# Two attention blocks on one core: wider exponentials, four-way PE tiles, exponentials by bit pattern, and orders written by a list scheduler

## The chip, the cores and the metric

The kernel runs on one core of one Trainium2 chip. The metric is the device time of one execution in microseconds (us), the median of the runs shown. The core has five engines with a queue each: PE (TensorE: matmuls, and the loading of weights, PEld), ACT (ScalarE), DVE (VectorE), POOL (GpSimd) and SP (SyncE, which here only issues DMAs). Matmuls write PSUM, which has eight banks of 512 float32 columns by 128 partitions.

## The reference, cut to what matters

Two independent attention blocks read 2048 tokens of width 448, with 16 heads of 28 columns, and their outputs are put side by side.

```python
# A: full attention, one key and one value head shared by all 16 query heads
q = (x @ wq).reshape(1, 2048, 16, 28).transpose(0, 2, 1, 3)
k, v = x @ wk, x @ wv
p = softmax(einsum("bhqd,bkd->bhqk", q, k) * 28 ** -0.5)
a = einsum("bhqk,bkd->bhqd", p, v) ... @ wo
# B: each token sees itself and 7 earlier tokens, two apart
idx = pos[:, None] - 2 * arange(8)[None, :]
logits = where(idx >= 0, q . k[idx] * 28 ** -0.5, -1e9)
b = (softmax(logits) . v[idx]) ... @ wo
out = concatenate([a, b], axis=-1)
```

A has 16 heads x 2048 queries x 2048 keys of scores. Laid out as keys on 128 partitions by 512 queries, one PSUM bank each, these are 1024 banks, and every one of their elements needs an exponential.

## The kernel before

The program is built by hand. A method adds items with a key (a period number and a rank), all items are sorted by key, and the sorted list gives each engine its order. Waits are written out item by item.

**A.** The loop has 512 periods p (`NPER`), one for each block of 128 keys (`tb`), pair of heads (`pair`) and chunk of 512 queries (`sc`). In a period PE makes the scores of two heads (`QK`, L693: two matmuls with 30 rows of the array each, at row positions 32 apart, into two banks). ACT takes the exponential of both banks in one instruction (`EXP`, L709, 128x1024) into one of three buffers `expT`. PE multiplies that by the values (`PV`, L730: two matmuls of 32 output rows at column positions 32 apart), which adds into one of two banks. The value tile has a column of ones, so row 28 collects the sum of the exponentials. Six of the eight banks belong to this loop: two slots of two banks for the scores, two for `PV`. Two rows beside the 28 of each head carry a bound on the score, taken from the squares of queries and keys, so that no exponential overflows.

The order on PE within a period is: wait for the last exponential (`FILLWAIT`), one step of other work or a filler, `PV(p-1)`, `QK(p+1)`. The other work (`_XTask`, `schedule_x`) has banks 6 and 7 and is placed by deadline: the query projections for the next chunk (L545), the projections of B (L621), the output projections (L853 for A, L1083 for B). Where nothing is due, `filler_item` (L1175) issues a matmul of the identity whose result nobody reads.

**B.** PE projects B's queries, keys and values (L621), DVE evicts them (L637), and the keys and values go to a scratch tensor in DRAM and come back eight times, shifted by two rows each (L911), so that all eight keys of a token lie on the token's own partition. Everything else is elementwise on DVE, in 16 blocks of 128 tokens: eight products (L930), four sums over the 28 columns (L940), maximum, subtraction, an exponential on ACT (L978), the weights, products with the values (L1004, L1012) and sums (L1031 to L1038). PE then transposes the result (L1056) and projects it.

**Start and end.** Before the loop, SP issues four transposing DMAs of A's input (L303) and, behind them on the same queue, the weights (L326 to L330). PE makes values, keys and the first queries, the bound is worked out, and the loop begins. After each chunk the sums go through small DMAs to 16 partitions (`den_sc`, L756), DVE takes the reciprocal (L769), PE spreads it (L811), DVE multiplies (L821), and the outputs are projected and stored.

Of the kernel before, what the change touches and what calls it, by code (L numbers as in the profile page):

```python
# [10 lines left out]
I32 = mybir.dt.int32  # L11

S = 2048
D = 448
H = 16
DH = 28
NSB = S // 128
SCALE = float(DH) ** -0.5
WIN = 8
NEG = -1.0e9  # L20

NSC = 4
NPAIR = 8
NTB = 16
NPER = NSC * NPAIR * NTB
NGRP = NSC * NPAIR

BANKW = 512
NWARM = 10
XGAP = 6  # L30


NKV = 2


def P1B(k):
    return 42 + 26 * k


class _Sem:  # L40
    def __init__(self, h, name):
        self.h = h
        self.name = name
        self.count = 0


class _Eng:

    def __init__(self, gen, name, engine):
        self.gen = gen  # L50
        self.name = name
        self.engine = engine
        self.thunks = []

    def w(self, sem, count):
        if count is None or count <= 0:
            return
        assert count <= sem.count, (
            f"{self.name}: wait on {sem.name}>={count} but only {sem.count} signalled so far (global order violation)"
        )  # L60
        eng = self.engine
        h = sem.h
        self.thunks.append(lambda: eng.wait_ge(h, count))

    def i(self, fn, sig=None, inc=1):
        eng = self.engine
        if sig is None:
            self.thunks.append(lambda: fn(eng))
            return None
        sig.count += inc  # L70
        h = sig.h
        self.thunks.append(lambda: fn(eng).then_inc(h, inc))
        return sig.count


class _XTask:
    def __init__(self, name, kinds, elig, deadline, slot_fn):
        self.name = name
        self.kinds = kinds
        self.nslots = len(kinds)  # L80
        self.elig = elig
        self.deadline = deadline
        self.slot_fn = slot_fn
        self.deps = []
        self.slots = []
        self.bank = None
        self.st = {}


class _Gen:  # L90
    def __init__(self, nc, A_x, A_wq, A_wk, A_wv, A_wo, B_x, B_wqkv, B_wo, out):
        self.nc = nc
        self.A_x, self.A_wq, self.A_wk, self.A_wv, self.A_wo = A_x, A_wq, A_wk, A_wv, A_wo
        self.B_x, self.B_wqkv, self.B_wo = B_x, B_wqkv, B_wo
        self.out = out
        self.items = []
        self._seq = 0

    def add(self, key, fn):
        self._seq += 1  # L100
        self.items.append((key, self._seq, fn))

    def sem(self, es, name):
        return _Sem(es.enter_context(self.nc.semaphore(name=name)), name)

    def bank(self, b, lo=0, n=BANKW):
        return self.ps[:, b * BANKW + lo: b * BANKW + lo + n]

    def bank_rows(self, b, r0, r1, lo=0, n=BANKW):
        return self.ps[r0:r1, b * BANKW + lo: b * BANKW + lo + n]  # L110

    def bank_bf(self, b, lo=0, n=2 * BANKW):
        return self.psb[:, b * 2 * BANKW + lo: b * 2 * BANKW + lo + n]

    def build(self):
        nc = self.nc
        with ExitStack() as es:
            self.alloc(es)
            self.plan()
            self.items.sort(key=lambda t: (t[0], t[1]))  # L120
            for key, seq, fn in self.items:
                fn()
            block = es.enter_context(nc.Block())
            E = self.E

            @block.gpsimd
            def _(eng):
                for t in E["gp"].thunks:
                    t()

            @block.sync
            def _(eng):
                for t in E["sp"].thunks:
                    t()

            @block.tensor
            def _(eng):
                for t in E["pe"].thunks:
                    t()

            @block.scalar
            def _(eng):
                for t in E["act"].thunks:
                    t()

            @block.vector
            def _(eng):
                for t in E["dve"].thunks:
                    t()

    def alloc(self, es):
# [5 lines left out]
        self.ps = es.enter_context(nc.psum_tensor("ps", [128, 8 * BANKW], FP32))  # L157
        self.psb = self.ps[:, :].bitcast(BF16)
        self.kv_dram = nc.dram_tensor("kv_scratch", (S, 2 * D), BF16)
# [3 lines left out]
        self.wqkv = sb([128, 4, 3 * D], BF16, "wqkv")  # L163
        self.qkv_q = sb([128, NSB, D], BF16, "qkv_q")
        self.kv_stage = sb([128, 2, 2 * D], BF16, "kv_stage")
        KS = WIN * 2 * D
        self.ARENA = NKV * KS + 2 * 8 * D + 6 * D
        self.arena = sb([128, self.ARENA], BF16, "arena")
        self.kT_rep = sb([128, S], BF16, "kT_rep")
        self.q_sq = sb([128, 4, 512], BF16, "q_sq")  # L170
        self.q_tmp = sb([128, 4, 512], BF16, "q_tmp")
        self.v_aug = sb([128, NTB, 32], BF16, "v_aug")
        self.qT = sb([128, 2, 4, 512], BF16, "qT")
        self.expT = sb([128, 3, 1024], BF16, "expT")
        self.PV_sb = sb([128, 2, 4, 512], FP32, "PV_sb")
        self.bsel4 = sb([16, 4, 128], BF16, "bsel4")
        self.oTn = sb([128, 2, 4, 512], BF16, "oTn")
        self.den_sc = sb([16, 2, 512], FP32, "den_sc")
        self.rden = sb([16, 512], FP32, "rden")
        self.rden_bf = sb([16, 512], BF16, "rden_bf")  # L180
        self.kmax = sb([128, 4], FP32, "kmax")
        self.cols = sb([128, 8], FP32, "cols")
        self.cols_i = sb([128, 1], I32, "cols_i")
        self.wq_pad = sb([128, 4, 512], BF16, "wq_pad")
        self.wq_raw = sb([128, 4, D], BF16, "wq_raw")
        self.wk4 = sb([128, 4, 128], BF16, "wk4")
        self.wv_pad = sb([128, 4, 32], BF16, "wv_pad")
        self.wo4 = sb([128, 4, D], BF16, "wo4")
        self.wo_B = sb([128, 4, D], BF16, "wo_B")
        self.ident = sb([128, 128], BF16, "ident")  # L190
        self.halfblk = sb([128, 128], BF16, "halfblk")
        self.ones8 = sb([128, 128], BF16, "ones8")
        self.mask_add = sb([128, H, WIN], FP32, "mask_add")
        self.lg = sb([128, H, WIN], FP32, "lg")
        self.lgm = sb([128, H, WIN], FP32, "lgm")
        self.lg2 = sb([128, 2, H, WIN], FP32, "lg2")
        self.mx = sb([128, H], FP32, "mx")
        self.e_t = sb([128, 2, H, WIN], FP32, "e_t")
        self.ssum = sb([128, H], FP32, "ssum")
        self.rs = sb([128, H], FP32, "rs")  # L200
        self.a_n = sb([128, H, WIN], BF16, "a_n")
        self.o_bf = sb([128, 8, D], BF16, "o_bf")
        self.oT_sb = sb([128, 3, 512], BF16, "oT_sb")
        self.outB = sb([128, 2, D], BF16, "outB")
        self.outA = sb([128, 2, D], BF16, "outA")

        ar = self.arena
        self.KV = [ar[:, r * KS:(r + 1) * KS].rearrange("p (w c) -> p w c", w=WIN) for r in range(NKV)]
        self.Ksh = [kv[:, :, 0:D] for kv in self.KV]
        self.Vsh = [kv[:, :, D:2 * D] for kv in self.KV]  # L210
        o = NKV * KS
        self.prod = ar[:, o:o + 8 * D].rearrange("p (w c) -> p w c", w=8)
        o += 8 * D
        self.prod2 = ar[:, o:o + 8 * D].rearrange("p (w c) -> p w c", w=8)
        o += 8 * D
        self.S4 = ar[:, o:o + 4 * D].rearrange("p (w c) -> p w c", w=4)
        self.S2 = ar[:, o + 4 * D:o + 6 * D].rearrange("p (w c) -> p w c", w=2)
        o += 6 * D
        assert o == self.ARENA, o
        self.kT_raw = ar[:, 1 * KS: 1 * KS + S]  # L220
        self.k_sq = ar[:, 1 * KS + S: 1 * KS + S + 4 * 512].rearrange("p (t c) -> p t c", t=4)
        assert 1 * KS + S + 4 * 512 <= 2 * KS

        self.sem_xa = self.sem(es, "in_xa")
        self.sem_xb = self.sem(es, "in_xb")
        self.sem_wa = self.sem(es, "in_wa")
        self.sem_wb = self.sem(es, "in_wb")
        self.sem_wo = self.sem(es, "in_wo")
        self.pe_qk = self.sem(es, "pe_qk")
        self.pe_pv = self.sem(es, "pe_pv")  # L230
        self.pe_x = self.sem(es, "pe_x")
        self.act_a = self.sem(es, "act_a")
        self.act_x = self.sem(es, "act_x")
        self.dve_a = self.sem(es, "dve_a")
        self.dve_b = self.sem(es, "dve_b")
        self.dve_x = self.sem(es, "dve_x")
        self.gp_s = self.sem(es, "gp_s")
        self.gp_b = self.sem(es, "gp_b")
# [1025 lines left out]
```

## Time and profile before

| | us |
|---|---|
| runs | 627.05, 628.19, 627.03; median 627.05 |
| span of the profiled execution | 627.4 (0.35 above the median) |
| first exponential of the loop starts | 59.3 |
| last wait for the sums before the final outputs (DMA `den_sc`) | 606.4 to 608.1 |
| PE busy / ACT busy / DVE busy / POOL busy | 549.7 / 507.3 / 360.3 / 22.3 |

One page of the profile shows one execution. "Busy" is the time covered by an engine's instructions; a matmul's end is modelled, so a PE that is busy all the time need not be at its best. A line of the groups gives the source line, the engine, what it writes and reads, its shape and count, then busy time and mean duration of one, then the idle time of the engine just before them and what ended it. The chain follows the work that ended last back to the start. The mean clock granted to PE was 0.986.

### The profile page before, as it was taken

To read this page: it belongs to the slowest core of one execution; us is meant where nothing else is said; L and a number is where in the kernel's file an instruction comes from. 1 tells how busy PE (TensorE), PEld (TensorE's weight loads), DVE (VectorE), ACT (ScalarE), POOL (GpSimd) and SP (SyncE) were. 2 spreads that over 40 slices of the span, in tenths; PEclk is the share of its full clock that TensorE was granted. 3 is DMA by queue.
4 is the path that set the end of the run, shared out by engine and by line. 5 is a ranking of instruction groups with operands and counts; after the bars stand their busy time and mean duration, and the time that the engine had idled before them with its cause. 6 is when DMAs were issued, how large, how long until landed. Compare 5 with 4: busy or idle time off the path is not lost.

```text
span 627.4 us, 7987 instructions
## 1 busy us (share of the span) xinstructions
PE 549.7 (88%) x2831; PEld 167.4 (27%) x2878; DVE 360.3 (57%) x600; ACT 507.3 (81%) x538; POOL 22.3 (4%) x42
## 2 busy tenths in 40 slices
PE   0295999999999998999999989999999999999956
PEld 0121222222222222222222222222222222222312
DVE  2114114687656767885766777777665977521135
ACT  0032888898888889998889999989989999999950
POOL 5006200000000000000000000000000000000000
PEclk9997999999999999999999999999999999999987
DMA  9920030430124043030223140303314030000001
GB/s 198 150 52 11 29 109 35 132 113 20 45 91 147 16 132 118 1 117 2 68 87 98 43 140 2 117 32 110 112 37 139 9 126 15 16 30 16 16 8 59
DMA packets 46461, 43.89 MB, mean 70 GB/s; under 512 B 22943, under 2 KB 46087, under 8 KB 46423
## 3 DMA queue, kind: packets, MB, share of 16 engines
q1 hardware_dynamic: 45447, 41.39, 22.7%
q0 software_dynamic: 976, 2.01, 1.3%
q8 instruction: 22, 0.36, 0.2%
q14 instruction: 16, 0.13, 0.1%
HBM read 31.72 MB, written 7.34 MB: 62 GB/s over the span
## 4 chain that ended last, share of the span: by engine, by line
PE 66%; ACT 21%; issue 4%; DVE 4%; SPq 3%; DMA 1%; ACTq 0%; DVEq 0%
ACT expT L709 21%; PE ps L730 20%; PE ps L693 19%; PE ps L621 8%; PE ps L1175 7%; PE ps L1083 3%; PE ps L853 2%; SPq L303 2%; PE ps L545 2%; PE ps L455 1%; PE ps L472 1%; PE ps L433 1%; PE ps L1056 1%; SPq L326 1%; DVE lg L940 1%
## 5 line engine op out<-in xcount | busy, mean ns | idle before, releaser
L709 ACT ACTIVATE expT<-ps 128x1024 bf16<-128x1024 f32 x512 | 498.7, 1022 | 56.0 <-PE ps L693 52.9
L730 PE MATMUL ps<-expT,v_aug 128*32 128x512 bf16 x1024 | 201.2, 389 | 23.0 <-ACT expT L709 13.3
L693 PE MATMUL ps<-qT,kT_rep 30*128 30x512 bf16 x1024 | 198.8, 385 | 0.0
L1175 PE MATMUL ps<-kT_rep,ident 128*128 128x512 bf16 x216 | 84.2, 390 | 9.9 <-ACT expT L709 8.8
L730 PEld LDWEIGHTS ps<-expT,v_aug 128*32 128x32 bf16 x1024 | 49.2, 92 | 136.6 <-ACT expT L709 70.2
L693 PEld LDWEIGHTS ps<-qT,kT_rep 30*128 30x128 bf16 x1024 | 48.3, 91 | 116.1 <-issue 116.1
L940 DVE TENSOR_REDUCE lg<-arena 128x32 f32<-128x896 bf16 x64 | 66.6, 1079 | 0.5
L621 PE MATMUL ps<-wqkv,xT_B 128*128 128x448 bf16 x192 | 58.0, 360 | 0.0
L1012 DVE TENSOR_TENSOR arena<-arena,a_n 128x1344 bf16<-128x1344 bf16 (+1 forms) x32 | 56.7, 1784 | 0.0
L637 DVE CAST kv_stage<-ps 128x448 bf16<-128x448 f32 x32 | 19.9, 622 | 45.5 <-PE ps L621 45.4
L1175 PEld LDWEIGHTS ps<-kT_rep,ident 128*128 128x128 bf16 x256 | 24.6, 96 | 69.2 <-ACT expT L709 53.3
L930 DVE TENSOR_TENSOR arena<-qkv_q,arena 128x448 bf16<-128x448 bf16 x128 | 40.8, 383 | 0.0
L749 DVE COPY PV_sb<-ps 64x512 f32<-64x512 f32 x32 | 21.8, 681 | 22.3 <-PE ps L730 21.6
L637 DVE CAST qkv_q<-ps 128x448 bf16<-128x448 f32 x16 | 10.0, 625 | 38.8 <-PE ps L621 38.8
L433 PE MATMUL ps<-wv_pad,xT_A 128*128 128x32 bf16 x64 | 5.4, 198 | 27.8 <-DVE cols L379 27.8
L438 ACT ACT_TABLE_LOAD x1 | 1.3, 1283 | 33.3 <-PE ps L433 33.3
L865 DVE CAST outA<-ps 128x448 bf16<-128x448 f32 x16 | 10.0, 623 | 29.9 <-PE ps L853 29.7
L1094 DVE CAST outB<-ps 128x448 bf16<-128x448 f32 x16 | 10.0, 622 | 29.7 <-PE ps L1083 29.6
L621 PEld LDWEIGHTS ps<-wqkv,xT_B 128*128 128x128 bf16 x192 | 14.5, 96 | 31.5 <-issue 30.8
L1083 PE MATMUL ps<-wo_B,oT_sb 128*128 128x448 bf16 x64 | 22.2, 374 | 0.3 <-DVE outA L865 0.3
L853 PE MATMUL ps<-wo,oTn 128*128 128x448 bf16 x64 | 21.3, 371 | 0.0
L769 DVE RECIPROCAL rden<-den_sc 16x512 f32<-16x512 f32 x4 | 13.4, 3338 | 9.9 <-DMA den_sc<-PV_sb 9.9
(86 smaller groups left out, 242.7 us busy)
## 6 DMA issues: line engine op xcount, KB each, us to landing
arena<-kv_scratch SPq DMA_DIRECT2D x121, 224.0 KB, 3.8
kv_scratch<-kv_stage SPq DMA_DIRECT2D x16, 224.0 KB, 1.9
out_dram<-outB SPq DMA_DIRECT2D x16, 112.0 KB, 1.7
out_dram<-outA SPq DMA_DIRECT2D x16, 112.0 KB, 1.7
den_sc<-PV_sb SPq DMA_DIRECT2D x64, 2.0 KB, 1.7
wqkv<-in_B_wqkv_dram POOLq DMA_DIRECT2D x3, 336.0 KB, 5.3
wo<-in_A_wo_dram POOLq DMA_DIRECT2D x16, 24.5 KB, 1.8
wo_B<-in_B_wo_dram POOLq DMA_DIRECT2D x3, 112.0 KB, 6.1
```

The lines of the kernel that those rows point to most:

```text
L621: c = pe.i(lambda e, b=b, lhsT=lhsT, rhs=rhs, kt=kt, tp=tp: e.matmul(g.bank(b, 0, D), lhsT, rhs, start=(kt == 0), stop=(kt == 3), tile_pos ...
L637: cd = dve.i(lambda e, b=b, dst=dst: e.tensor_copy(out=dst, in_=g.bank(b, 0, D)), g.dve_x)
L693: c = pe.i(lambda e, slot=slot, j=j, lhsT=lhsT, rhs=rhs, base=base: e.matmul(g.bank(2 * slot + j), lhsT, rhs, start=True, stop=True, tile_ ...
L709: c = act.i(lambda e: e.activation(g.expT[:, ering, :], g.ps[:, 1024 * slot:1024 * slot + 1024], ACT.Exp, scale=SCALE), g.act_a)
L730: c = pe.i(lambda e, j=j: e.matmul(g.bank_rows(pvb, 32 * j, 32 * j + 32), g.v_aug[:, tb, :], g.expT[:, ering, 512 * j:512 * (j + 1)], star ...
L749: c = dve.i(lambda e: e.tensor_copy(out=g.PV_sb[r0:r0 + 64, dpar, t, :], in_=g.bank_rows(pvb, 0, 64)), g.dve_a)
L853: c = pe.i(lambda e, b=b, t=t: e.matmul(g.bank(b, 0, D), g.oTn[:, sc % 2, t, blk4 * 128:(blk4 + 1) * 128], g.wo4[:, t, :], start=(t == 0), ...
L930: c = dve.i(lambda e: e.tensor_tensor(out=g.prod[:, w, :], in0=Q, in1=Kw, op=ALU.mult), db)
L940: c = dve.i(lambda e: e.tensor_reduce(out=g.lg[:, :, 2 * q4:2 * q4 + 2].rearrange("p h w -> p w h"), in_=g.prod[:, 2 * q4:2 * q4 + 2, :].r ...
L1012: c = dve.i(lambda e: e.tensor_tensor(out=g.prod2[:, w0:w1, :].rearrange("p w (h d) -> p w h d", d=DH), in0=Vw, in1=g.a_n[:, :, w0:w1].rea ...
L1083: c = pe.i(lambda e, b=b, lhsT=lhsT, rhs=rhs, i=i, tp=tp: e.matmul(g.bank(b, 0, D), lhsT, rhs, start=(i == 0), stop=(i == 3), tile_positio ...
L1175: pe.i(lambda e: e.matmul(g.bank(slotb), g.ident[:, :], g.kT_rep[:, 0:512], start=True, stop=True))
```

## The change

The file is a new program with the same interface. Its parts:

- **Orders.** Every instruction is an operation with the tiles that it reads and writes. The builder keeps a clock for each engine and a table of costs, always lets the engine that is furthest behind choose (`pe_choose`, `act_choose`, `spec_choose`), and appends the choice to that engine's order. Waits follow from the tiles (`emission`). On the chip each engine runs its order in sequence.
- **A's scores.** The same 1024 matmuls, of 29 rows each, now go out in groups of up to four at the four row positions. Their banks are a ring of three (0, 1, 2), a ring of two (3, 4), and for a fourth score one of the flexible banks 5, 6, 7. There are 330 such groups.
- **Exponentials.** ACT takes one ring at a time: 182 instructions of 128x1536 and 183 of 128x1024, 912 banks in all, 848 of A and 64 of B. The other 176 banks of A go to DVE: an addition and a maximum write the score, scaled so, as a 16-bit integer that is the bit pattern of a bf16 power of two (`Z`, L1155). Two more additions (L1163 128x512, L1170 128x1024) make three shifted copies, on POOL 134 times and on DVE 42 times. `PV` adds the four copies, each with its own scaled value tile, so such a bank costs four matmuls (704 in all) where another costs one (848).
- **B.** Its queries are ordered by parity, so that the eight keys of a token are neighbours. A mask is put into two banks by a matmul with the identity, the scores of five blocks of some 103 queries by 110 keys are added for two heads, ACT takes the exponential of both banks, and PE multiplies by the values (`bpv`). The scratch tensor for keys and values and all of B's elementwise work on DVE are gone.
- **Projections.** They are made in groups of four tiles of 32 output rows at the four column positions (`proj4`, L512), so each former matmul is four.
- **Division.** For each of 32 groups of four heads: DVE copies the bank out, four DMAs lay the four rows of sums over 128 partitions, DVE takes the reciprocal, a DMA writes it to DRAM, another reads it spread over the partitions, and POOL (24 times) or DVE (8 times) multiplies (`chain`).
- **Start.** The first 512 rows of A's input are loaded untransposed and transposed on PE; the rest comes by 28 smaller transposing DMAs. The first weights are issued from ACT's queue. Fillers are gone, apart from eight matmuls at the start.

The diff, cut to its core:

```diff
-        def QK(p):
...
-                for j in range(2):
-                    base = (pair % 2) * 64 + 32 * j
...
-                c = act.i(lambda e: e.activation(
-                    g.expT[:, ering, :], g.ps[:, 1024 * slot:1024 * slot + 1024], ACT.Exp, scale=SCALE), g.act_a)
...
+WJ = (0.240234375, 0.2021484375, 0.169921875, 0.142578125)
...
+        self.rings = [[0, 1, 2], [3, 4]]
+        self.flex = [5, 6, 7]
...
+                self.put("act", lambda e: e.activation(g.P[:, k, 0:512 * n], g.ps[:, lo:lo + 512 * n], ACT.Exp, scale=ASCALE), ns, ns + 110,
+                         [self.banks[b].res for b in banks], self.pslotres[k][0:n], name="exp")
...
+    def do_qk(self, jobs, kind, reads):
...
+            def em(e):
+                for b in ring:
+                    ins = e.matmul(g.bank(b), g.ident[:, :], (g.mask if half else g.mask0)[:, :], start=True, stop=False)
+                return ins
...
+            for (gr, tb, j), b in zip(alljobs, banks):
+                ins = e.matmul(g.bank(b), g.kT_A[32 * j:32 * j + DH + 1, 128 * tb:128 * tb + 128],
+                               g.qT_A[32 * j:32 * j + DH + 1, gr.sc % 2, gr.g, :], start=True, stop=True, tile_position=(32 * j, 0))
...
+    def dread(self, job, bank):
...
+            return dict(emit=lambda e: e.tensor_scalar(out=g.Z[:, z, 0, :], in0=g.bank(bank.i), scalar1=ZBIAS, scalar2=0.0, op0=ALU.add, op1=ALU.max),
+                        reads=[bank.res], writes=[zr[0]], took=ns + 95, cb=cb)
...
+            return dict(emit=lambda e: e.tensor_scalar(out=g.Z[:, z, 1, :], in0=g.Z[:, z, 0, :], scalar1=32.0, scalar2=None, op0=ALU.add),
+                        reads=[zr[0]], writes=[zr[1]], took=ns + 60, cb=cb)
...
+            return dict(emit=lambda e: e.tensor_scalar(out=g.Z[:, z, 2:4, :], in0=g.Z[:, z, 0:2, :], scalar1=64.0, scalar2=None, op0=ALU.add),
+                        reads=[zr[0], zr[1]], writes=[zr[2]], took=ns + 60, cb=cb)
...
+    def do_pv(self, picks):
...
+        def em(e):
+            for b, j, l, r, st, sp in mm:
+                ins = e.matmul(g.bank(b, 32 * j, 32 * j + 32), l, r, start=st, stop=sp, tile_position=(0, 32 * j))
+            return ins
...
+    def proj4(self, bank, lhs, rhs, n, mrows=None, start=True, stop=True):
+
+        def emit(e):
+            for j in range(4):
+                m = 32 if mrows is None else mrows(j)
+                ins = e.matmul(self.bank(bank, 32 * j, 32 * j + m, 0, n), lhs(j), rhs(j), start=start, stop=stop, tile_position=(0, 32 * j))
+            return ins
...
-            def ff():
-                pe.i(lambda e: e.matmul(g.bank(slotb), g.ident[:, :], g.kT_rep[:, 0:512], start=True, stop=True))
-            self.add((p, 5), ff)
```

## The prediction

> **What bounds the kernel now.** I read the page first (busy times, slices, chain), then the groups, then the timeline of one stretch in the middle.
>
> ```profile
> span 627.4 us, 7987 instructions
> PE 549.7 (88%) x2831; PEld 167.4 (27%) x2878; DVE 360.3 (57%) x600; ACT 507.3 (81%) x538; POOL 22.3 (4%) x42
> ...
> ACT  0032888898888889998889999989989999999950
> ...
> PE 66%; ACT 21%; issue 4%; DVE 4%; SPq 3%; DMA 1%; ACTq 0%; DVEq 0%
> ...
> L709 ACT ACTIVATE expT<-ps 128x1024 bf16<-128x1024 f32 x512 | 498.7, 1022 | 56.0 <-PE ps L693 52.9
> L730 PE MATMUL ps<-expT,v_aug 128*32 128x512 bf16 x1024 | 201.2, 389 | 23.0 <-ACT expT L709 13.3
> L693 PE MATMUL ps<-qT,kT_rep 30*128 30x512 bf16 x1024 | 198.8, 385 | 0.0
> L1175 PE MATMUL ps<-kT_rep,ident 128*128 128x512 bf16 x216 | 84.2, 390 | 9.9 <-ACT expT L709 8.8
> ```
>
> The loop runs from 59.3 (first exponential) to about 606: 547 us over 512 periods, 1.068 each. ACT waits for L693, and the chain lies on PE for two thirds. Why PE takes a microsecond for five matmuls shows in the timeline (start, duration):
>
> ```profile
> 300.00 0.39 PE L693 MATMUL ps<-qT,kT_rep 30*128 30x512 bf16 x2
> ...
> 300.32 0.39 PE L1175 MATMUL ps<-kT_rep,ident 128*128 128x512 bf16 x1
> 300.43 1.99 ACT L709 ACTIVATE expT<-ps 128x1024 bf16<-128x1024 f32 x2 [0.21 <-PE ps L693]
> ...
> 300.64 0.39 PE L730 MATMUL ps<-expT,v_aug 128*32 128x512 bf16 x2
> ...
> 300.97 0.39 PE L693 MATMUL ps<-qT,kT_rep 30*128 30x512 bf16 x2
> ```
>
> Three steps start 320 ns apart, whether a step is one matmul or two side by side. So a period needs 960 on PE, and some 1180 where the other step is two matmuls of L621; ACT, ready every 920 at the shortest spacings in the trace, mostly waits. Ahead of the loop lie 59 us, behind it 21.
>
> **What the Trainium skill says.**
> - "TensorEngine Tiling (Array Packing)", Key Properties: a change of tiling mode drains PE. The trace agrees: 320 between starts across a change, 217 to 220 between 128-row matmuls of 512 columns in one mode (L497), so a change costs 103.
> - "TensorE: Matmul & The Clock Gate", Measured speedup vs the span model: tiles in different positions start about 4 ns apart, yet four row tiles gained 3.07 times, not four. The trace shows 3 to 4 ns for pairs, and a pair at no more than the step of a single matmul. Groups of four it does not show.
> - "ScalarE: Activation LUTs", What ACT_TABLE_LOAD costs: 186 ns plus 0.833 per column, and neighbours overlap by 93. The trace has 1022 for 1024 columns, 597 for 512 (L479) and a spacing of 920: slope 0.83, overlap 102. I use the trace.
> - "GPSIMD Engine Reference", Elementwise: 1.03 cycles per element for up to two operations, 1.8 for a tight unrolled loop, 2.6 for two inputs, at 1.2 GHz. By this page my estimates are 0.86, 1.5 and 2.17 ns per element. The trace has a fill at 0.85 (L403, 6061 ns for 7168) and 308 ns for an affine select of 128 columns, so 0.2 us is fixed.
>
> **ACT.** 182 exponentials of 1536 columns: 920 + 425 (half of 1024 at the measured slope) = 1345 each, 244.8 us. 183 of 1024 at 920: 168.4. Sum **413** against 512 x 1068 = 547. This takes the 176 banks away (about 75 us of ACT at 425), adds 64 of B (27), drops the 16 small exponentials (4.9 busy) and saves the fixed part of 147 instructions.
>
> **PE**, from the new order's counts. Packs of up to four, unchanged in price from a pair (217 per 512 columns, 190 per 448, as L853 repeats) plus 10 for the further tiles:
> - A's scores, 330 groups x 225: 74
> - `PV`, 1552 matmuls in some 455 packs x 227: 103
> - projections and norms, 876/4 packs x 227 and 832/4 x 200: 50 + 42
> - B's masks 64 x 217, scores 32 x 250, `bpv` 80 packs x 60: 14 + 8 + 5
> - value projections of A, warm-up, transposes: 10
> - 757 changes of mode x 103: 78
>
> Sum **384**, of which some 15 lie before the first exponential or after the last. So PE has 369 of work under ACT's 413. Gone are 256 fillers and half of the mode changes (about three a period before, 1536).
>
> **DVE.** L930 to L1038 and L637 go. New: 176 reads of scores at 689 (as L559 casts 512 columns from PSUM) = 121; 42 pairs of shifts at about 354 + 488 (754 for 2048 columns at L512, less a quarter cycle for each column missing) = 35; 32 bank copies at 681, 32 output casts at 623, some 83 evictions at 625 to 690, 32 reciprocals at 253, the rest: 125. Sum 281 against 360: covered.
>
> **POOL**, nearly idle before. 134 pairs: 1536 x 0.86 + 0.4 = 1.72 us, 231. 24 multiplications and 20 squares at 512 x 2.17 + 0.2 = 1.31: 58. Setup 22: fills, some 30 selects at 0.3 and the issue of 12 weight loads at 0.55 that move to its queue; until then DVE makes the shifts. Sum 311; at 1.5 per element, 442. Covered at the first price, the bound at the second.
>
> **SP and DMA.** 286 issues instead of 262; at 0.57 (two at L756 took 1.14) some 165 us of SP, plus 28 transposes at 2.96/4 (L303 issued four in 11.85). The 41 MB on the queue shrink to a small part. Each of the 32 divisions is a chain: copy 0.7, four issues 2.3 and landing 1.7, reciprocal 0.3, two more transfers at 2.3, multiplication 0.7 to 1.3: 10 to 11 us, against 13 between groups (413/32) with three buffers. It is hidden, except at the end.
>
> **New waits.** PE waits for POOL's copies ahead of a `PV`, and the next scores are queued behind it, so ACT waits too. Likewise for DVE's evictions ahead of a projection. A turn of a ring (exponential ends, 100 ns, scores 430 until ACT starts: 300.22, 300.43) fits under the other ring's 920 to 1345 only if PE comes within 400 to 800 ns. Its packs of 217 with mode changes don't always allow that: I take 5% of 413, **20**, with 0 and 50 as ends.
>
> **Start.** SP issues four loads by 3.1, landed at 4.8; the weights from ACT's queue, behind the 1.28 table load, are issued by 5 and land 4 to 8 us later (3.9 alone, 8.2 behind transposes at L330). Then four cold packs at 430, eviction 0.7, square 0.43, norm 0.8, addition 0.75, scores 0.43: first exponential at 13 to 18, taken as **16** against 59.3. **End:** last `PV` and the chain, 11; projection of four blocks 3.4, cast 0.6, store 2.3: **17** against 21.
>
> **Sum.** 16 + 413 + 20 + 17 = **466 us** in the span, and 466 for the metric, since the span before was 0.35 above its median.
>
> **The rivals.**
> 1. *PE becomes the bound.* By 3.07 a pack of four costs 4 x 217/3.07 = 283. On 330 + 455 + 427 packs that is 55 more each, 67 us: PE 451, of which 436 in the loop. With two engines at their limit and ACT's 5% on top, 33 + 436 + 30 = **499**. For it: only pairs are shown, and PE has just 10% to spare. Against: a second tile was free.
> 2. *POOL is late.* At 1.5 per element its 442 exceed ACT's 413, and PE, in order, waits for it: 25 (its setup) + 420 + 17 and stalls of 40 to 80 make **500 to 545**. If all of the affine select's 308 ns were per element, 2.4, a pair would take 3.69: 494 + 58 + 39 = 591. For it: no elementwise operation on integers, and none of 512 columns, is in POOL's trace. Against: the fill runs at 0.85.
> 3. *Slower: groups of four don't run side by side.* The place is every pack on PE, L1119, L1218 and L512. It decides from (594 - 369)/1212 = 186 ns more a pack, where 594 is 627 less start and end. Two steps a pack, as if the array took tiles in pairs, cost 217 more: 369 + 263 + 33 = **665**. For it: no group of four is in the trace, and four times the weight loads go through one port (91 ns each at L693). Against: the two loads and two matmuls of a pair all start within 4 ns, and the step of a pair is no longer than that of one.
>
> **Chances.** Forecast 0.60 (440 to 490), first rival 0.20, second 0.13, third 0.06, no change 0.01 (a chance meeting of these). Low end: first exponential at 13, no stalls, end 14: 440. High end: the second rival's 545; above it lie POOL at its dearest and the third rival. Forecast and two rivals are faster: 0.93. Within 0.2%, about what a measurement of this kernel can tell from no change: 0.01.
>
> **What would show it.** In the changed profile: spacings of neighbouring exponentials at 1345 and 920; the first near 16; ACT busy above 85% between; packs of four starting some 12 ns apart and 320 after the step of another mode; L1163 and L1170 on POOL near 0.64 and 1.08. The forecast is wrong if ACT's idle time exceeds 50 us; behind L1119 with PE full it is the first rival, with `PV` waiting for Z the second.

## The result, and the profile after

The changed kernel takes **715.7 us** (median of 4 runs, 713.5 to 723.0) against 627.3 before (4 runs, 627.0 to 628.2): ratio 1.142, interval 1.136 to 1.149. It is slower by a seventh, where 466 was forecast. A few executions of any of these kernels show a lower granted clock and are up to 3% longer than the others: two of the four of e7 below, and the profiled one of e2.

The page of the changed kernel: span, busy times, two rows of slices, the chain by engine and by line, and four groups.

```profile
span 713.4 us, 12414 instructions
...
PE 503.2 (71%) x5268; PEld 141.2 (20%) x5268; DVE 290.6 (41%) x496; ACT 433.5 (61%) x369; POOL 642.5 (90%) x369
...
POOL 7799949999699999998799999998999999999960
PEclk9988978886987678569989969677576865555556
...
POOL 80%; PE 11%; issue 4%; DVE 3%; DMA 1%; POOLq 0%; ACTq 0%; ACT 0%; SPq 0%
POOL Z L1170 48%; POOL Z L1163 26%; PE ps L512 4%; POOL oTn L778 3%; PE ps L1218 3%; POOL sq L652 3%; PE ps L1119 2%; DVE Z L1155 1%; DMA bc<-rec_scratch 1%; DMA wq<-in_A_wq_dram 1%; PE ps L1078 1%; DVE qT_A L658 0%; PE ps L1092 0%; DVE PVs L728 0%; DVE ob L818 0%
...
L924 ACT ACTIVATE P<-ps 128x1536 bf16<-128x1536 f32 x365 | 431.0, 1247 | 253.4 <-PE ps L1119 204.4
L1170 POOL TENSOR_SCALAR Z<-Z 128x1024 int16<-128x1024 int16 x134 | 372.9, 2783 | 9.3
L1218 PE MATMUL ps<-Z,vA 128*32 128x512 bf16 x704 | 193.9, 493 | 126.7 <-POOL Z L1163 80.4
L1163 POOL TENSOR_SCALAR Z<-Z 128x512 int16<-128x512 int16 x134 | 201.4, 1503 | 21.3 <-DVE Z L1155 21.3
```

Before, POOL was busy 4% of the span; now it is the fullest engine at 90%, at 9 in most slices, and the chain lies on it for 80%. Two lines make this: the shifts L1163 and L1170. Each mean is more than twice the 0.64 and 1.08 us that the prediction asked for. Their durations have medians of 1.487 and 2.768 us; 134 pairs are 574 us, products and squares another 51. ACT, the engine that was to be the bound, stands idle for 253 us ahead of L924.

ACT's line names the scores (L1119, PE) as what it waits for, not POOL. The link is in the timeline of one stretch in the middle (start, duration, engine, and in brackets how long it waited and for whom):

```profile
299.80 1.49 POOL L1163 TENSOR_SCALAR Z<-Z 128x512 int16<-128x512 int16 x1
301.37 2.77 POOL L1170 TENSOR_SCALAR Z<-Z 128x1024 int16<-128x1024 int16 x1
304.11 1.49 POOL L1163 TENSOR_SCALAR Z<-Z 128x512 int16<-128x512 int16 x1
...
305.65 0.61 PE L1218 MATMUL ps<-Z,vA 128*32 128x512 bf16 x2 [7.27 <-POOL Z L1163]
```

POOL runs one shift after the other without a gap. PE needs the copy that L1163 makes, gets it at 305.6, and has stood for more than 7 us. PE runs its order in sequence, so the scores behind that `PV` stood too, and behind them both readers of scores. The waits, in us in total, times, and the longest:

```profile
DVE Z L1155 <- PE ps L1119: 223.0, 122, 8.7
ACT P L924 <- PE ps L1119: 204.4, 109, 8.6
PEld ps L1218 <- POOL Z L1163: 103.0, 37, 7.8
```

Two engines wait 200 us each "for PE", and PE waits for POOL. Read alone, their lines look like PE's fault; the third line shows what PE was waiting for.

In the same trace much of the forecast holds. The first exponential starts at 12.9. The four matmuls of a pack start within some 10 ns, at 216 to 227 from the pack before in the same mode and 320 to 325 across a change. Exponentials that don't wait start 1330 to 1347 after one of 1536 columns and 903 to 920 after one of 1024.

### The profile page after: what moved, and what is told of

Its sections match the earlier page's. It is cut to its first block, busy times and chain, and to the rows that moved or that the text cites. A ratio compares the mean times of both kernels' runs of the same rounds, so it can differ in the third digit from the quotient of the medians.

```text
span 713.4 us, 12414 instructions
## 1 busy us (share of the span) xinstructions
PE 503.2 (71%) x5268; PEld 141.2 (20%) x5268; DVE 290.6 (41%) x496; ACT 433.5 (61%) x369; POOL 642.5 (90%) x369
## 4 chain that ended last, share of the span: by engine, by line
POOL 80%; PE 11%; issue 4%; DVE 3%; DMA 1%; POOLq 0%; ACTq 0%; ACT 0%; SPq 0%
POOL Z L1170 48%; POOL Z L1163 26%; PE ps L512 4%; POOL oTn L778 3%; PE ps L1218 3%; POOL sq L652 3%; PE ps L1119 2%; DVE Z L1155 1%; DMA bc<-rec_scratch 1%; DMA wq<-in_A_wq_dram 1%; PE ps L1078 1%; DVE qT_A L658 0%; PE ps L1092 0%; DVE PVs L728 0%; DVE ob L818 0%
## 5 line engine op out<-in xcount | busy, mean ns | idle before, releaser
L924 ACT ACTIVATE P<-ps 128x1536 bf16<-128x1536 f32 x365 | 431.0, 1247 | 253.4 <-PE ps L1119 204.4
L1170 POOL TENSOR_SCALAR Z<-Z 128x1024 int16<-128x1024 int16 x134 | 372.9, 2783 | 9.3
L1218 PE MATMUL ps<-Z,vA 128*32 128x512 bf16 x704 | 193.9, 493 | 126.7 <-POOL Z L1163 80.4
L1163 POOL TENSOR_SCALAR Z<-Z 128x512 int16<-128x512 int16 x134 | 201.4, 1503 | 21.3 <-DVE Z L1155 21.3
L1218 PE MATMUL ps<-P,vA 128*32 128x512 bf16 x848 | 191.6, 471 | 30.7 <-POOL Z L1170 18.1
L1155 DVE TENSOR_SCALAR Z<-ps 128x512 int16<-128x512 f32 x176 | 121.0, 688 | 223.4 <-PE ps L1119 223.0
L1119 PE MATMUL ps<-qT_A,kT_A 29*128 29x512 bf16 x1024 | 157.1, 465 | 12.1 <-DVE Z L1155 3.9
L1218 PEld LDWEIGHTS ps<-Z,vA 128*32 128x32 bf16 x704 | 40.2, 101 | 190.3 <-POOL Z L1163 87.1
L1119 PEld LDWEIGHTS ps<-qT_A,kT_A 29*128 29x128 bf16 x1024 | 34.4, 94 | 165.3 <-issue 80.2
L1218 PEld LDWEIGHTS ps<-P,vA 128*32 128x32 bf16 x848 | 40.7, 98 | 86.1 <-issue 40.7
L512 PE MATMUL ps<-xT_B,wB 128*32 128x512 bf16 x512 | 51.2, 447 | 1.0 <-DVE kT_B L688 0.8
L728 DVE COPY PVs<-ps 128x512 f32<-128x512 f32 x32 | 21.8, 687 | 49.9 <-PE ps L1218 35.5
L512 PE MATMUL ps<-woA,oTn 128*32 128x448 bf16 x256 | 26.8, 473 | 17.6 <-POOL oTn L778 17.4
L1170 DVE TENSOR_SCALAR Z<-Z 128x1024 int16<-128x1024 int16 x42 | 28.3, 675 | 0.9
L512 PE MATMUL ps<-wB,xT_B 128*32 128x448 bf16 (+3 forms) x320 | 27.6, 413 | 0.2 <-DVE PVs L728 0.2
L1163 DVE TENSOR_SCALAR Z<-Z 128x512 int16<-128x512 int16 x42 | 26.2, 623 | 1.1
L512 PE MATMUL ps<-woB,oTn 128*32 128x448 bf16 x256 | 21.9, 406 | 5.3 <-POOL oTn L778 4.6
L512 PE MATMUL ps<-xT_A,wq 128*32 128x512 bf16 x256 | 23.3, 428 | 0.6 <-DMA wq<-in_A_wq_dram 0.4
```

The lines of the kernel that those rows point to most:

```text
L512: ins = e.matmul(self.bank(bank, 32 * j, 32 * j + m, 0, n), lhs(j), rhs(j), start=start, stop=stop, tile_position=(0, 32 * j))
L728: return dict(emit=lambda e: e.tensor_copy(out=g.PVs[:, p, :], in_=g.bank(bank.i)), reads=[bank.res], writes=[self.pvs.res[p]], took=ns + ...
L924: self.put("act", lambda e: e.activation(g.P[:, k, 0:512 * n], g.ps[:, lo:lo + 512 * n], ACT.Exp, scale=ASCALE), ns, ns + 110, [self.banks ...
L1119: ins = e.matmul(g.bank(b), g.kT_A[32 * j:32 * j + DH + 1, 128 * tb:128 * tb + 128], g.qT_A[32 * j:32 * j + DH + 1, gr.sc % 2, gr.g, :], s ...
L1155: return dict(emit=lambda e: e.tensor_scalar(out=g.Z[:, z, 0, :], in0=g.bank(bank.i), scalar1=ZBIAS, scalar2=0.0, op0=ALU.add, op1=ALU.max ...
L1163: return dict(emit=lambda e: e.tensor_scalar(out=g.Z[:, z, 1, :], in0=g.Z[:, z, 0, :], scalar1=32.0, scalar2=None, op0=ALU.add), reads=[zr ...
```

## The experiments

Theories at the start. **T1:** POOL's shifts, at 2.5 ns per column, are the bound, and PE's fixed order hands their lateness on. **T2:** the dense packs pull down the clock granted to PE (0.756 in this profile; the row `PEclk` falls to 5 and 6 near the end), and this is what everyone waits for. **T3:** the planned orders are at fault whatever POOL costs. **T4:** POOL is slow only because DVE works in the same memory at the same time. For each run "ACT's waits" are the time from the first to the last exponential less what the exponentials need at 1347 and 904 ns each.

| kernel | us, median | ratio to before, 95% | first exp. | ACT's need | ACT's waits | tail |
|---|---|---|---|---|---|---|
| after | 715.7 | 1.142 (1.136-1.149) | 12.9 | 410.6 | 268.0 | 21.9 |
| e1_dve_shifts | 474.1 | 0.755 (0.751-0.760) | 12.7 | 411.0 | 24.9 | 21.5 |
| e2_priced | 539.6 | 0.856 (0.849-0.862) | 12.8 | 416.4 | 93.3 | 23.0 |
| e3_no_bits | 574.7 | 0.915 (0.907-0.923) | 12.8 | 489.8 | 44.9 | 21.6 |
| e4_fp32_view | 522.2 | 0.832 (0.828-0.836) | 12.8 | 410.6 | 74.8 | 21.9 |
| e5_no_bits_fill | 548.6 | 0.875 (0.866-0.884) | 13.3 | 489.8 | 24.7 | 21.4 |
| e6_dve_fill | 475.0 | 0.757 (0.751-0.762) | 14.5 | 413.3 | 22.0 | 21.5 |
| e7_two_banks | 521.0 | none given | 12.7 | 398.7 | 84.2 | 22.4 |
| e8_short_shifts | 489.5 | 0.781 (0.774-0.788) | 12.6 | 410.6 | 43.8 | 21.8 |
| e9_dve_all_prices | 479.2 | 0.760 (0.757-0.764) | 13.1 | 415.1 | 26.8 | 21.6 |
| e10_squares_dve | 472.0 | 0.751 (0.749-0.753) | 13.0 | 414.2 | 16.6 | 22.4 |
| e11_dve_old_prices | 482.5 | 0.768 (0.766-0.771) | 12.5 | 411.9 | 32.8 | 22.7 |
| e12_pool_beside | 483.3 | 0.768 (0.766-0.770) | 13.0 | 411.0 | 36.0 | 21.8 |

### Taking the shifts off POOL: e1_dve_shifts

```diff
-self.later(("gp", "dve"), (GP_S1, 215), [zr[0]], sh1, ..., hold=True, ...)
+self.later(("dve",), (290,), [zr[0]], sh1, ...)
-self.later((eng,), (ns * 1.7,), [zr[0], zr[1]], sh2, ...)
+self.later(("dve",), (410,), [zr[0], zr[1]], sh2, ...)
```

> The changed program, but all shifts of Z (L1163, L1170) go to DVE and none to POOL; the list scheduler is told 290 and 410 ns for them and plans its orders anew. Theory 1, POOL's shifts are the bound (134 pairs of 4.26 us, 574 of the 713 us, and PE waits for them in order): POOL busy falls from 642 to about 100 us, DVE rises to about 380, ACT sets the pace, 445 to 485 us, and the clock of TensorE returns above 0.95, since PE no longer sits idle for microseconds. Theory 2, four-way tiles draw TensorE's clock down to 0.756 and PE is slow by itself: the clock stays below 0.85 and the time above 600. Theory 3, orders planned ahead do not hold on the chip whatever the shifts cost: 520 to 600, with ACT idle over 100 us.

Measured: 474.1 us, 24.5% under the kernel before. Its page:

```profile
PE 409.1 (87%) x5246; PEld 131.0 (28%) x5262; DVE 351.1 (75%) x741; ACT 420.2 (89%) x370; POOL 94.5 (20%) x118
...
ACT  2789999999999999998979999998799899999920
...
PEclk9899999999999999999969999999799898999876
...
ACT P L924 40%; PE ps L1218 8%; PE ps L512 7%; PE ps L1119 6%; DMA bc<-rec_scratch 4%; DVE Z L1155 4%; DVE Z L1170 3%; DMA den<-PVs 3%; DVE Z L1163 2%; PE ps L1078 2%; SPq L214 2%; PE ps L1092 2%; DVE qT_A L658 1%; POOL oTn L778 1%; DMA rec_scratch<-rec 1%
...
L1218 PE MATMUL ps<-Z,vA 128*32 128x512 bf16 x696 | 148.9, 406 | 2.8 <-DVE Z L1163 1.6
```

With POOL at 20%, ACT is at 9 in nearly every slice and carries the largest part of the chain; `PV` of Z waits 3 us where it waited 127; a matmul of L1218 takes 406 ns in the mean where it took 493, with the clock back at 0.952. T1 is confirmed, and T2 loses its ground: the packs are as dense and the clock is high.

### The same orders with a cheaper shift: e4_fp32_view and e8_short_shifts

e1 also changed the orders, since the scheduler planned anew. These two keep the orders of the changed kernel. The first lets POOL see the same bytes as half as many fp32 numbers; the second cuts each POOL shift to 16 columns, 32 for L1170. So in both runs the copies that POOL makes lack the shift, or most of it; they serve to show the time alone.

```diff
-e.tensor_scalar(out=g.Z[:, z, 1, :], in0=g.Z[:, z, 0, :], scalar1=32.0, ...)
+e4: out=g.Z[:, z, 1, :].bitcast(FP32), in0=g.Z[:, z, 0, :].bitcast(FP32), scalar1=0.0   (on POOL)
+e8: out=g.Z[:, z, 1, 0:16], in0=g.Z[:, z, 0, 0:16]                                      (on POOL)
```

> The orders of the changed kernel instruction for instruction, but POOL's two shifts treat the same bytes as half as many fp32 numbers and add zero, so the shifted copies made on POOL are not shifted. Only POOL's price changes. Theory 1 with a price per element: L1163 about 0.22 + 256 x 2.5 = 0.86 us, L1170 1.5, POOL busy 380, and the kernel at 450 to 500 us with the clock back above 0.95. If the integer type alone is dear and fp32 is cheaper still (0.86 per element): 0.44 and 0.66, 445 to 480. Theory 4, POOL's time is spent waiting for the port that it shares with DVE: both stay near 1.49 and 2.77, and the time near 713. Theory 2: the clock stays low whatever POOL does.

> The orders of the changed kernel instruction for instruction, with POOL's two shifts cut to 16 and 2 x 16 columns (the rest of those shifted copies stays zero, from six extra fills on DVE of about 0.8 us each near the start). Only POOL's price changes, to about 0.25 and 0.3 us. Theory 1, and the rest of the prediction's sum is right: 455 to 480 us, first exponential near 13, ACT's idle time in the loop below 45 us, clock above 0.93. Theory 3, the planned order is itself at fault: above 505, with ACT still idle for more than 70.

The groups of e4, then the busy times and groups of e8:

```profile
L1170 POOL TENSOR_SCALAR Z<-Z 128x512 f32<-128x512 f32 x134 | 201.1, 1501 | 9.2
...
L1163 POOL TENSOR_SCALAR Z<-Z 128x256 f32<-128x256 f32 x134 | 115.3, 861 | 55.6 <-DVE Z L1155 55.0
```

```profile
PE 421.8 (86%) x5268; PEld 133.6 (27%) x5268; DVE 270.4 (55%) x502; ACT 421.0 (86%) x369; POOL 148.2 (30%) x369
...
L1167 POOL TENSOR_SCALAR Z<-Z 128x16 int16<-128x16 int16 x134 | 34.9, 261 | 199.2 <-DVE Z L1159 199.2
...
L1174 POOL TENSOR_SCALAR Z<-Z 128x32 int16<-128x32 int16 x134 | 39.8, 297 | 9.2
```

By the records' medians 256 fp32 columns take 0.849 us and 512 take 1.489, the same as 512 int16 columns (1.487) in the changed kernel; 1024 take 2.768. With e8's 0.25 and 0.29 for 16 and 32 columns, all lie on one line: **0.21 us + 2.50 ns per column**, whatever the type. The cost of this operation is by element, not by byte. T4 falls too: in the changed kernel 38 of the 134 L1163 have no DVE instruction beside them at all, and they took 1.486 us in the mean against 1.503 for all; even in e12, where DVE is 77% busy, the mean of such an addition rises only to 1.62.

The times follow POOL's load: 715.7, 522.2 and 489.5 us at 642, 386 and 148 us of POOL. In e4 POOL's 386 are already less than ACT's 411, and ACT still waits 75: on a path that PE walks in order, a POOL copy that comes late costs time even when POOL isn't full. e4's durations came as expected and its time missed the 450 to 500. e8 missed its expectation of 455 to 480: orders that were planned around wrong times lose 43.8 us of ACT where e1's lose 24.9. So T3 is true in part, at the price of some 15 us against a loss of 240.

### Telling the scheduler the true prices: e2_priced

```diff
-GP_S1 = 560.0;  GP_TT16 = 620.0;  GP_TT32 = 1150.0
+GP_S1 = 1490.0; GP_TT16 = 1040.0; GP_TT32 = 1275.0
-(GP_S1, 215) ... (ns * 1.7,)
+(GP_S1, 290) ... (2770.0 if eng == "gp" else 410.0,)
```

> The changed program with nothing but the scheduler's prices altered: POOL's shifts at 1490 and 2770 ns, its squares at 1040 and products at 1275, DVE's shifts at 290 and 410. It then gives POOL 70 pairs of shifts and DVE 93 (134 and 42 before), and 13 fewer banks go the way of bit patterns. Theory 1: POOL 70 x 4.26 + 60 = 360 us busy and no longer the bound, 455 to 500 us. Theory 2: above 600 with a clock below 0.85. Theory 3: 520 to 600. If DVE's shifts and POOL's lie in each other's way at SBUF, DVE's take well over the 277 and 378 ns of their fastest, and the time lies above that of the run with all shifts on DVE.

The scheduler now leaves 70 pairs on POOL and puts 93 on DVE. Measured: 539.6 us, 40 above the range expected under T1, inside the one under T3, and 65 above e1, which has POOL make none. The profiled execution was the longest of the four (545.6 in the span), so its split is rough. POOL is busy 345 us there and no bound by itself; a scheduler that knows the price repairs the kernel only in part. Three things can be behind it: the planned orders (T3), POOL's copies, which take 4.3 us behind the read where DVE's take 0.7, and what POOL does to DVE beside it (e12, below; here the 66 shifts of 512 columns that DVE starts under a POOL shift take 547 ns in the mean, and the 17 with POOL at rest 286). How the 65 us divide among them was not settled.

### No bits at all, and the clock: e3_no_bits and e5_no_bits_fill

```diff
-DRATE = 0.25
+DRATE = -1.0        # all 1088 banks to ACT
+e5 also: in pe_choose, where PE would idle 217 ns or more and a flexible bank is free,
+    self.pe_op("col", self.proj4(b, ident, kT_A, 512), 217.0, ..., name="filler")
```

> The changed program without exponentials by bit pattern: all 1024 banks of A and the 64 of B go to ACT, 218 instructions of 1536 columns and 217 of 1024. Everything else of the change stays: four-way tiles, B on PE, the planned orders. At the spacings in the changed kernel's trace, 1347 and 903 ns: 294 + 196 = 490 us of ACT, with 13 ahead and 17 to 22 behind and 5 to 20 of waits 525 to 545 us. Theory 1: just that, with a clock above 0.95. Theory 2: four-way packs still throttle TensorE, clock below 0.85, over 600. Theory 3: 560 to 640, ACT idle over 60 us in the loop.

> The run without bit patterns (575 us, TensorE at 0.713 of its clock) with fillers: where the scheduler finds nothing for PE but has room, it puts in a pack of four matmuls whose result nobody reads, some 560 packs. More work, none of it useful. Theory 5, the granted clock falls because PE is idle too often, not because its packs are dense: the clock rises above 0.93 and the time falls to 525 to 550 us, near the 540 that the sum of exponentials gave. Theory 2, dense packs draw the clock down: the clock falls further and the time rises above 580. If fillers only stand in the way of the scores, the clock rises and the time stays at 570 to 585.

Busy times and granted clock of e3, then of e5:

```profile
PE 487.7 (86%) x4724; PEld 132.8 (23%) x4740; DVE 115.2 (20%) x220; ACT 501.1 (88%) x439; POOL 91.9 (16%) x117
...
PEclk9899958765889996858969965555755755555555
```

```profile
PE 511.7 (93%) x6980; PEld 164.1 (30%) x6980; DVE 116.0 (21%) x220; ACT 496.9 (90%) x439; POOL 92.4 (17%) x117
...
PEclk9899999799899999899999999999999999999986
```

e3 missed the 525 to 545 us and the high clock of T1: its `PEclk` drops to 5 in the second half, with a mean of 0.713, though it has no Z and fewer matmuls. With some 560 filler packs the mean is 0.972 and the kernel is 26 us **faster**. So the clock falls where PE has too little to do, not too much, the opposite of T2.

The clock records say this slot by slot. They hold only full and half clock (so a mean of 0.713 is a mixture), and they change on a grid of 3.41 us. The 14 profiles, each without its first 20 and last 25 us, have 1619 such slots at full clock. After 130 of them the clock fell to half, and PE was busy at most 73% of each of those; after the 1409 busier ones it never fell; of the 64 in which PE was busy half the time or less, all but one were followed by a fall. In the changed kernel 33 slots were followed by a fall, the busiest at 62%, and of the 171 us that PE was idle there for over 1 us at a time, 148 ended with one of POOL's shifts. That its low clock follows from this waiting is thus shown; what the low clock then added to its time no run took alone. The Trainium skill, "TensorE: Matmul & The Clock Gate", Part 1: The HAM clock gate, says that idle stretches lower the clock; the runs agree, though in e3 no single idle time of PE was long: before the tail the longest is 2.3 us, and PE stands at 86% busy by the page (at a low clock a matmul counts longer).

e5 and e1 together price the bits themselves: from e5 to e1 174 banks go from ACT to DVE, ACT's need falls by 78.8 us, the span of the profiles by 79.0 and the median by 74.5. What ACT gives up is gained nearly whole.

### What is left in e1: e6, e7, e9, e10, e11

```diff
e6: e1 + the fillers of e5 (some 115 packs)
e7: e1 with   self.rings = [[0, 1], [3, 4]];  self.flex = [2, 5, 6, 7]
e9: e1 with   GP_TT16 = 1040.0;  GP_TT32 = 1275.0
e10: e1 with  GP_TT32 = 1275.0 and all squares on ("dve",)
e11: e1 with  (215,) and (365.5,) for DVE's shifts, as the changed kernel has them
```

> All shifts on DVE (474 us) with the same kind of fillers, some 115 packs, since here PE has little room. Theory 5: the clock rises from 0.952 to 0.97 or more, and with fewer late scores the time falls by 3 to 12 us, 462 to 471. If the remaining waits are the handshake of PE and ACT and not the clock: 472 to 478.

> All shifts on DVE, with two rings of two banks, so that every exponential has 1024 columns, and the bank set free joins the flexible ones. At spacings of 903 against 1347 for three banks, ACT's sum hardly changes: 457 x 903 = 413 us against 411. If the width serves the turn of the ring, as the prediction's working has it (530 ns of turn under 903 instead of 903 and 1347, with one mode change more per exponential on PE, 92 more groups of scores at 320): 485 to 520 us. If three banks save only the fixed part of an instruction: 472 to 480.

> As e1_dve_shifts, and the scheduler is also told what POOL's squares and products take (1040 and 1275 ns where it was told 620 and 1150); it then puts 3 of the 32 products on DVE and 166 banks instead of 174 on DVE's bits, so ACT has 8 banks (3.4 us) more. If the 25 us that ACT still waits in e1 come from work that is planned too early on POOL: 460 to 470. If they come from elsewhere: 474 to 480.

> As e1_dve_shifts, with all squares on DVE (in e1 29 of 32 are on POOL) and the product's price told right; 167 banks of bits, 3 us more for ACT. If DVE's shifts are held by POOL's work, fewer are held, and the norms are no longer late: 464 to 473, with fewer than 20 shifts of 512 columns near 0.6 us (30 in e1). If POOL's rest does not matter: 474 to 480.

> As e1_dve_shifts, but the scheduler is told the old prices of DVE's shifts (215 and 365 ns, where e1 has 290 and 410). e8_short_shifts, with the old orders, loses 44 us of ACT where e1 loses 25. If the old DVE prices are the cause: 482 to 492. If it is not they but the orders planned around POOL: 472 to 479.

e6: 475.0, as e1, though the clock rose from 0.952 to 0.970. There is nothing left to win from fillers.

e7, busy times:

```profile
PE 463.7 (90%) x5352; PEld 133.9 (26%) x5352; DVE 368.2 (71%) x831; ACT 419.5 (81%) x447; POOL 94.9 (18%) x118
```

441 exponentials of 1024 instead of 366 of both sizes, and yet ACT's need is 12 us less, since more banks went to DVE. What rose is the wait, 84 instead of 25, and so it isn't the saved fixed part that makes the third bank of a ring worth having. Of e7's executions those with the higher clock took 512.6 and 520.0, 39 and 46 us above e1. Two causes of the waits remain: a ring gives PE less time to come round (904 ns of cover instead of up to 1347), and PE itself, now 90% busy, has 77 groups of scores and 130 changes of mode more (by estimate 77 x 0.225 + 130 x 0.103 = 31 us). They weren't told apart.

e9: right prices for POOL's squares and products gave 479.2, not 460 to 470, and the waits are no fewer (26.8), so they come from elsewhere. e10 is the fastest median of all, 472.0, inside its range; its interval overlaps e1's, so the gain over e1 isn't shown by the time alone. By the profile it is there and is small: ACT waits 16.6 instead of 24.9, and needs 3.2 more for seven banks that came back to it.

```profile
ACT P L924 61%; PE ps L512 7%; PE ps L1119 5%; PE ps L1218 5%; DMA den<-PVs 2%; DMA bc<-rec_scratch 2%; SPq L214 2%; DVE Z L1155 2%; DMA wq<-in_A_wq_dram 1%; DVE Z L1163 1%; DVE qT_A L658 1%; DVE ob L818 1%; PE ps L1078 1%; POOL oTn L778 1%; DVE PVs L728 1%
```

61% of the chain now is L924: ACT itself. e11 gave 482.5, and 8 us more waits than e1: of the 19 us of waits by which e8 exceeds e1, DVE's old prices explain 8. The other 11 stay open; e8's orders also plan for POOL's shifts, but no run took that alone.

### POOL working beside DVE: e12_pool_beside

In e1 the timeline shows one shift after another (start, duration):

```profile
103.41 0.43 DVE L1170 TENSOR_SCALAR Z<-Z 128x1024 int16<-128x1024 int16 x1
...
105.52 1.04 POOL L652 TENSOR_TENSOR sq<-qT_B 128x512 bf16<-128x512 bf16 x1 [3.18 <-DVE qT_B L658]
105.68 1.17 DVE L1170 TENSOR_SCALAR Z<-Z 128x1024 int16<-128x1024 int16 x1
```

A shift of 1024 columns takes 0.43 us. The one that starts 0.16 us after a square on POOL takes 1.17 and ends 0.29 after it. In e1, 15 of the 18 shifts of 512 columns, and 19 of the 19 of 1024, that start while POOL has a square or product under way end 0.15 or 0.28 us after that instruction; those that start before POOL's are not held. The test keeps e1's orders and gives POOL extra work:

```diff
+self.idle = sb([128, 2, 512], I16, "idle")
 def cb(o):                       # when DVE has read a bank of scores
     unit(0, zr[0])
+    if self.nD % 2 == 0:
+        pace = Res(); pace.w.append(o)
+        self.put("gp", e.tensor_scalar(out=idle[:, 1, :], in0=idle[:, 0, :], scalar1=32.0, ...), reads=[pace, ...])
```

> As e1_dve_shifts with the same orders on PE, ACT and DVE; POOL makes 87 additions of 512 int16 columns more, each released by a DVE read of scores, into a tile that nobody reads (130 us of POOL, which is then 48% busy). If POOL's work holds DVE's shifts (614 ns beside POOL, 285 without, in e1): half or more of the 174 first shifts stand near 0.6 us, DVE is busy 30 to 50 us longer, and ACT waits 10 to 30 us more: 484 to 505. If the long shifts beside POOL were chance: shifts stay near 0.29, and only POOL's squares and products come later by up to 1.5 us each: 472 to 480.

Busy times, POOL's extra additions, and DVE's shifts L1163 (here L1170):

```profile
PE 416.2 (86%) x5246; PEld 132.8 (28%) x5262; DVE 373.1 (77%) x742; ACT 421.4 (87%) x370; POOL 235.7 (49%) x205
...
L1159 POOL TENSOR_SCALAR idle<-idle 128x512 int16<-128x512 int16 x87 | 141.3, 1624 | 135.2 <-DVE Z L1162 134.3
...
L1170 DVE TENSOR_SCALAR Z<-Z 128x512 int16<-128x512 int16 x174 | 75.5, 444 | 2.1
```

Measured: 483.3 us, 9.2 above e1 with the intervals apart; DVE is busy 22 us longer, and ACT waits 11 more. The first theory is right in kind and was put somewhat too high: 484 was its low end, DVE was to be busy 30 to 50 us longer, and half of the 174 shifts were to be held. The reason is in the records: a shift of 512 columns that starts under one of POOL's one-input additions takes 466 ns in the mean (52 of them), under a square or product 1009 (22, every one held to POOL's end), under neither 327 (285 at the median). The Trainium skill, "SBUF — State Buffer", Who interferes with whom, says that DVE and POOL share a pair of ports, that DVE operations of some kinds, `tensor_scalar` among them, can use it, and that then whichever of the two starts first gets the pair for the whole instruction and the other blocks fully. For POOL's two-input operations the runs agree; beside its one-input additions only 8 of 52 shifts waited to the end, and many were not held at all, so there the measurement decides. Some of the 9 us may be squares and products that come later behind the extra additions.

## Why the prediction was wrong

**The step that failed** is one term: "134 pairs: 1536 x 0.86 + 0.4 = 1.72 us, 231". Measured: 1536 x 2.50 + 2 x 0.21 = 4.26, and 4.29 in the mean, 574 us. The fixed part was right; the price per column was three times too low. It came from "GPSIMD Engine Reference", Elementwise, of the Trainium skill (1.03 cycles per element, by estimate 0.86 ns), with a fill in the trace at 0.85 taken for agreement. A fill reads nothing. The only operation in the trace of before in which POOL reads, works and writes was the affine select: 286 to 313 ns for 128 columns of bf16, and 416 for the one of fp32. If nothing of it were fixed, the 308 ns are 2.4 per column and the 416 are 3.25. The first stood in the second rival as the dearest end and was left outside the range; the second was overlooked. Not that the select is the right price: in the changed kernel selects of 4 columns take 0.19 us, so those of 128 cost some 0.9 a column in bf16 (by estimate, (307 - 194)/124), near the fill. No row of before held the price of an addition. The measurement refutes the page's price for this operation.

**The second rival** named the right mechanism, in order: POOL late, PE waiting in sequence, `PV` waiting for Z. It got 0.13 and ended at 545 because it was worked out at 1.5 per element. e4 comes near that case: POOL at 386 us, 522 measured. Its dearest sum, 591, was itself too low: beside shifts, products and setup it has only the tail, 17, where the changed kernel's span holds 713.4 - 642.5 = 71 beside POOL's busy time. With the measured 71, and the measured 68 for squares, products and setup, by this estimate the case turns slower than 627 at (627 - 71 - 68)/134 = 3.64 us a pair. The prediction's 3.69 is already there: the slower side was within reach of its second rival, and it was given to another mechanism alone.

**Refuted rivals.** Four tiles do run side by side (third rival: starts within some 10 ns), and a pack of four costs 216 to 227 ns, not the 283 of the first rival; in e1 PE's share of the chain is smaller than ACT's, and ACT waits only 25 us.

**The rest of the sum** can be read from e1, in which POOL's part is gone:

| term | predicted | e1 |
|---|---|---|
| first exponential | 16 | 12.7 |
| ACT | 413 | 411.0 |
| waits | 20 | 24.9 |
| tail | 17 | 21.5 |
| span | 466 | 470.2 |

So 466 was about the time of this program with its shifts on DVE; the change gains what it was said to gain on ACT, and POOL took it and more. On DVE 281 stood against 290.6 measured, in part by luck: its 42 pairs of shifts took 54.5 us instead of 35, and the rest 236 instead of 246. Squares and products were somewhat dear at 1.31 us each: 1.04 and 1.27 were measured. The tail was missed by 4 to 6 us in every version. The 466 against e1's 470 hides a start that came 3.3 us earlier, and waits and a tail that together were 9.4 longer.

## What to carry to other kernels

Before work is moved to an idle engine, price it by a row of that engine with the same operation; neither a fill nor a select was a price for an addition, and where no such row exists, the price is unknown and the range has to hold the dearest reading of what there is. Then turn the question round: at which price does this engine become the bound, and does that reading reach it? If the next matmul in a fixed order reads the moved result, its latency counts as well as its load: here, taking the shifts back to a DVE that was 41% busy gives a kernel that needs 34% less time than the one that spread them.

When an engine waits for PE, look at what PE waits for; and a falling granted clock can be the result of waiting rather than its cause.

## What the runs showed of the hardware

- POOL's addition of a constant costs 0.21 us + 2.50 ns per column of 128 partitions, for int16 from 16 to 1024 columns and for fp32 at 256 and 512. A product of two bf16 tiles of 512 columns takes 1.04 us, of two fp32 tiles 1.27.
- DVE makes the same int16 addition of 512 columns in 0.285 us and of 1024 in 0.42, unless POOL is under way with a two-input operation: then 34 of 37 in e1 end 0.15 or 0.28 us after POOL's instruction.
- A matmul pack of four tiles costs the step of one matmul, 216 to 227 ns for 512 columns.
- Filler matmuls raised the mean granted clock from 0.713 to 0.972 and gained 26 us (e3, e5); at 0.952 they gained nothing (e1, e6). In 14 profiles the clock fell to half after 130 slots of 3.41 us, all with PE busy at most 73%, and after none of the 1409 busier ones.
